# Attention on one core: GpSimd's pieces of a seven-tile batch handed out 2, 1, 1, 1, 1, 1 instead of 1, 1, 1, 1, 1, 2

## The chip, the cores and the metric

One core of a Trainium2 chip runs the whole kernel in one launch. The metric is the device time of one execution in microseconds (us), the median of several runs. Five engines work side by side and wait for each other by semaphores: TensorE (PE in the profile, its weight loads PEld), VectorE (DVE), ScalarE (ACT), GpSimd (POOL) and the queue that issues most DMAs (SP).

## The reference

Two kinds of layer alternate, spectral, attention, spectral, attention, each on a layer norm of x and with a residual. The change is in the attention layers, so only they are shown:

```python
B, S, D, H = 1, 2048, 512, 32          # Dh = 16, one key head shared by all 32 query heads
q = (x @ wq).reshape(B, S, H, Dh).transpose(0, 2, 1, 3)
k, v = x @ wk, x @ wv
scores = einsum("bhqd,bkd->bhqk", q, k) * Dh ** -0.5
o = einsum("bhqk,bkd->bhqd", softmax(scores), v)
return o.transpose(0, 2, 1, 3).reshape(B, S, H * Dh) @ wo
```

A spectral layer is an rfft2, a product with complex weights, and the inverse, written as matmuls.

## The kernel before

**Groups and tiles.** An attention layer works on 32 groups of 64 score tiles. A group `g` is four query heads and a block of 512 queries; its 64 tiles are 16 key blocks by 4 heads, each tile 128 keys by 512 queries. Every tile has to be exponentiated and multiplied with the values on TensorE (`pv`, L648).

**Two ways to the exponential.** Of the 64 tiles 45 go through ScalarE: TensorE writes scores into `sc` (L546), ScalarE's Exp reads them into `e` (L635), alternately three and two tiles at once. The other 19 go through VectorE in three batches, `DPOS`: 6, 7 and 6 tiles. VectorE turns a score tile `dv` into a 16-bit pattern by one multiply and add (`t_new`, L669, "the pass" below), whose bits are read as bf16. Such a pattern stands for a coarse exponential; it is made finer by adding four shifted copies of it, the images, with the weights `PH_W`. Image 0 is `t_new` itself. Images 1 and 2 are made by VectorE, the whole batch in one instruction (`s_new`, L684). Image 3 is made by GpSimd, one tile at a time: these are the pieces (`pool_new`, L688). Each tile of each image is a matmul of its own on TensorE.

**Steps.** The order is laid down by hand: a loop over steps `n`, one ScalarE Exp each, 18 steps for a group. In each step the instructions are recorded as `act_step`, `dv_score`, `dv_pass`, `image_step`, `pv_step`, and `chain()` pins the order on TensorE, ScalarE, VectorE and GpSimd. A batch `b` of group `g` has six image steps, k = 0 to 5 (`BSTEPS`), which begin at step 6b of the group. VectorE's image 1 comes at k = 0 and image 2 at k = 3 (`IMG`). The pieces were dealt out over k = 0 to 5 by `share`, which for seven tiles gives 1, 1, 1, 1, 1, 2.

**What a piece waits for.** `pace` (L550) makes each piece wait for the latest VectorE image that has been recorded, `image[0]`. For k = 0, 1, 2 that is image 1, for k = 3, 4, 5 it is image 2. Nothing else holds a piece back to its step.

**Who reads a piece.** `pv_step` multiplies the images' tiles in the order image 0, 1, 2, 3, two steps (`LAG`) after their own share of the six steps. Of a seven-tile batch, tiles 0 and 1 of image 3 are due at step 12 of the group and tiles 2 to 6 at step 13; in some steps a projection piece (`piece_at`) puts the `pv` matmuls off. TensorE works in order: while a `pv` matmul waits, the scores recorded behind it, of the next Exp among them, wait too.

**Other work beside.** In the first image step of the seven-tile batch GpSimd also normalises the group before (`od_new`, L580, recorded behind that step's pieces). VectorE transposes that result for two groups at once (`ot_new`, L586, only in groups of even number), just ahead of image 2 of the seven-tile batch. It also casts the next group's queries (`qt`, L376 and L380).

In what follows "image (1)" and "image (2)" of the seven-tile batch are VectorE's instructions at k = 0 and k = 3, "the next image" is image (1) of the third batch, six steps on from image (1), and piece 0 to piece 6 are GpSimd's.

Of the kernel before, what the change touches and what calls it, by code (L numbers as in the profile page):

```python
# [26 lines left out]
BSTEPS = 6  # L27
# [330 lines left out]
class Attention:  # L358
# [70 lines left out]
    def run(self, row_done, work, psums):  # L429
# [55 lines left out]
        share = lambda total, k: range(total * k // BSTEPS, total * (k + 1) // BSTEPS)  # L485
        due = {}
        for n0 in range(NS):
            lst = []
            if n0 in d_phase:
                g, b, k, tiles = d_phase[n0]  # L490
                for f in share(4 * len(tiles), k):
                    j, i = divmod(f, len(tiles))
# [57 lines left out]
        def pace(ins):  # L550
            if image[0] is not None:
                tc.add_manual_dep(ins.ins, image[0].ins.name, mybir.DependencyInfo(
                    mybir.DependencyClass.Sync, mybir.DependencyReason.DATA), reason="pace")
# [118 lines left out]
        def image_step(n):  # L672
            if n in d_phase:
                g, b, k, tiles = d_phase[n]
                src, nt = tb[(g, b)].bitcast(I16), len(tiles)
                if k == 0:
                    pool_new = work.tile([P, NBT, 512], I16, tag="SP", bufs=2)
                    sb[(g, b, 3)] = pool_new
                if k in IMG:
                    i = 1 + IMG.index(k)  # L680
                    s_new = work.tile([P, NBT, 512], I16, tag="S", bufs=3)
                    sb[(g, b, i)] = s_new
                    lo = POOL2 if i == 2 else 0
                    image[0] = nc.vector.tensor_scalar(out=s_new[:, lo:nt, :], in0=src[:, lo:nt, :], scalar1=PH_OFF[i], scalar2=None, op0=ALU.add)  # L684
                    if lo:
                        pace(nc.gpsimd.tensor_scalar(out=s_new[:, 0:lo, :], in0=src[:, 0:lo, :], scalar1=1.0, scalar2=PH_OFF[i], op0=ALU.mult, op1=ALU.add))
                for i in share(nt, k):
                    pace(nc.gpsimd.tensor_scalar(out=sb[(g, b, 3)][:, i, :], in0=src[:, i, :],  # L688
                                                 scalar1=1.0, scalar2=PH_OFF[3], op0=ALU.mult, op1=ALU.add))

# [13 lines left out]
        for n in range(NS + LAG + 2):  # L704
            now[0] = n
            act_step(n)
            dv = dv_score(n)
            for fn in pending:
                fn()
            del pending[:]  # L710
            if n in evict_at:
                evict(evict_at[n])
            dv_pass(n, dv)
            for fn in todo.pop(n, ()):
                fn()
            image_step(n)
            for fn in todo_pool.pop(n, ()):
                fn()
            pv_step(n)
            if n in piece_at:  # L720
                piece(*piece_at[n])
            chain()
# [447 lines left out]
```

## Time and profile before

| | us |
|---|---|
| median of 3 runs | 1563.37 (1562.22 to 1563.38) |
| the profiled execution's own time | 1565.87 |
| its span, first to last instruction | 1564.1 |
| busy in the span: ScalarE | 1442.9 (92%) |
| VectorE | 1420.6 (91%) |
| TensorE | 1349.6 (86%) |
| GpSimd | 797.0 (51%) |

The two attention layers take from about 110 to 790 us and from about 870 to 1555 us of the span; the spectral layers lie ahead of each. A busy share is an average: what a stage could gain is read from its own waits. In a row of the timeline stand the start, the time taken, engine, line, operation, tiles and count; the bracket behind it is the idle time ahead of it and what ended that. Instructions of one kind that follow each other are merged into one row with a count.

### The profile page before, as it was taken

The page shows a single profiled execution, that of the slowest core. Times are in us where ns is not written, and L with a number is a line of the kernel's source. Part 1 is how long each engine was busy: PE and PEld are TensorE (multiplying, and loading weights), DVE is VectorE, ACT ScalarE, POOL GpSimd, SP SyncE. Part 2 cuts the span into 40 slices and gives each one's busy share as a digit, 9 for nine tenths or more (in the row PEclk, how much of TensorE's full clock was granted, in tenths as well). Part 3 has the DMA queues.
Part 4 walks back from the last instruction along what each step waited for, and adds up shares of the span by engine and source line. Part 5 has one row for each costly group of instructions (what it writes and reads, how often), then busy time and mean ns, then how long its engine had stood idle before and what let it go on. Part 6 is the DMA issues. An engine that isn't in the chain of part 4 may idle for free.

```text
span 1564.1 us, 33013 instructions
## 1 busy us (share of the span) xinstructions
PE 1349.6 (86%) x13145; PEld 429.5 (27%) x13252; DVE 1420.6 (91%) x2279; ACT 1442.9 (92%) x1361; POOL 797.0 (51%) x1310
## 2 busy tenths in 40 slices
PE   5888888899888988898889788888998899889987
PEld 2442222222222222222234322222222222222222
DVE  6687999999999999999987889999999999999995
ACT  6659999999999999999965799999999999999996
POOL 1003555565656655665600055556556656666564
PEclk9997999999999999999999899999999999999998
DMA  8000000000000000000010000000000000000000
GB/s 278 16 1 1 2 2 1 1 1 2 1 2 1 1 1 2 1 2 1 1 41 1 1 1 2 2 1 5 5 2 5 5 4 5 5 5 5 5 5 18
DMA packets 13198, 17.21 MB, mean 11 GB/s; under 512 B 5748, under 2 KB 10484, under 8 KB 12788
## 3 DMA queue, kind: packets, MB, share of 16 engines
q1 hardware_dynamic: 12660, 14.05, 2.7%
q8 instruction: 103, 1.69, 0.4%
q0 software_dynamic: 384, 1.05, 0.2%
q14 instruction: 51, 0.42, 0.1%
HBM read 13.00 MB, written 2.10 MB: 10 GB/s over the span
## 4 chain that ended last, share of the span: by engine, by line
DVE 35%; ACT 31%; issue 14%; PE 12%; POOL 4%; DVEq 0%; POOLq 0%; ACTq 0%
ACT e L635 30%; DVE t_new L669 16%; DVE s_new L684 9%; POOL pool_new L688 4%; PE pv_new L648 4%; PE sc L546 3%; DVE st L105 1%; PE new L203 1%; DVE o L565 1%; DVE qt L376 1%; DVE ot_new L586 1%; PE dv L546 1%; PE new L294 1%; PE new L242 1%; DVE dst L353 1%
## 5 line engine op out<-in xcount | busy, mean ns | idle before, releaser
L635 ACT ACTIVATE e<-sc 128x1536 bf16<-128x1536 f32 (+1 forms) x1158 | 1316.6, 1293 | 21.7 <-PE dv L546 17.4
L688 POOL TENSOR_SCALAR pool_new<-t_new 128x512 int16<-128x512 int16 x1204 | 748.5, 644 | 719.9 <-DVE s_new L684 630.4
L669 DVE TENSOR_SCALAR t_new<-dv 128x512 uint16<-128x512 f32 x1204 | 791.5, 677 | 76.3 <-PE dv L546 61.7
L648 PE MATMUL pv_new<-e,vaug 128*32 128x512 bf16 x2892 | 595.6, 389 | 0.0
L546 PE MATMUL sc<-qt,KT 32*128 32x512 bf16 x2892 | 459.2, 388 | 115.0 <-ACT e L635 108.5
L546 PE MATMUL dv<-qt,KT 32*128 32x512 bf16 x1204 | 455.3, 387 | 21.8 <-DVE t_new L669 20.2
L648 PE MATMUL pv_new<-s_new,vaug 128*32 128x512 bf16 x2408 | 422.5, 386 | 5.9 <-DVE s_new L684 5.9
L684 DVE TENSOR_SCALAR s_new<-t_new 128x3584 int16<-128x3584 int16 (+1 forms) x380 | 386.3, 1017 | 0.1
L648 PE MATMUL pv_new<-pool_new,vaug 128*32 128x512 bf16 x1204 | 299.8, 387 | 20.8 <-POOL pool_new L688 20.8
L546 PEld LDWEIGHTS <-KT 32*128 32x128 bf16 x4096 | 156.7, 91 | 561.0 <-issue 559.4
L648 PEld LDWEIGHTS <-vaug 128*32 128x32 bf16 x7708 | 154.3, 94 | 399.3 <-issue 368.3
L648 PE MATMUL pv_new<-t_new,vaug 128*32 128x512 bf16 x1204 | 232.7, 387 | 0.0
L370 PE MATMUL ps<-xz,wq_sb 128*128 128x512 bf16 x186 | 61.5, 386 | 4.1 <-DVE t_new L669 0.4
L565 DVE STREAM_TRANSPOSE o<-pv_new 128x512 f32<-128x512 f32 x64 | 45.2, 706 | 12.2 <-PE pv_new L648 12.2
L203 PE MATMUL new<-tab_F,xz 128*128 128x512 bf16 x186 | 48.2, 404 | 3.5 <-DVE xz L167 3.3
L376 DVE TENSOR_SCALAR qt<-ps,kq 128x512 bf16<-128x512 f32 x62 | 46.0, 742 | 1.2 <-PE ps L370 1.2
L105 DVE BATCH_NORM_STATS2 st<-x_sb 128x6 f32<-128x512 bf16 x64 | 42.9, 671 | 3.6 <-DMA x_sb<-in_A_x_dram 3.5
L580 POOL TENSOR_TENSOR od_new<-o,den 128x256 bf16<-128x256 f32 x62 | 38.5, 620 | 0.0
L267 DVE TENSOR_TENSOR m<-x_new,wt 128x1024 bf16<-128x1024 bf16 x32 | 20.7, 687 | 14.3 <-ACT x_new L243 14.3
L243 ACT CAST x_new<-new 128x1024 bf16<-128x1024 f32 x16 | 16.2, 1012 | 18.4 <-PE new L242 17.0
L370 PEld LDWEIGHTS <-wq_sb 128*128 128x128 bf16 x256 | 22.0, 97 | 31.5 <-issue 16.7
L336 PE MATMUL new<-G_new,t_new 128*128 128x512 bf16 x128 | 29.9, 379 | 0.5 <-DVE G_new L303 0.4
(106 smaller groups left out, 582.0 us busy)
## 6 DMA issues: line engine op xcount, KB each, us to landing
tab_F<-const_F SPq DMA_DIRECT2D x5, 640.0 KB, 11.7
x_sb<-in_A_x_dram SPq DMA_DIRECT2D x4, 512.0 KB, 4.8
t_new<-const_IE SPq DMA_DIRECT2D x2, 1024.0 KB, 7.3
rt<-in_A_w_r_dram SPq DMA_DIRECT2D x1, 1028.0 KB, 8.4
rt<-in_A_w_i_dram SPq DMA_DIRECT2D x1, 1028.0 KB, 12.7
t_new<-const_IO SPq DMA_DIRECT2D x2, 512.0 KB, 3.3
out_dram<-x_sb SPq DMA_DIRECT2D x8, 128.0 KB, 2.0
out_dram<-x_sb POOLq DMA_DIRECT2D x8, 128.0 KB, 2.3
```

What stands on the lines that cost most here:

```text
L105: self.nc.vector.bn_stats(st, x_ap)
L203: self.mm(ps, lhsT=z, rhs=tab, start=start and i == 0, stop=stop and i == len(mms) - 1)
L370: self.nc.tensor.matmul(ps, lhsT=self.aw["wq"][:, c, hg, :], rhs=self.xT[:, c, 4 * qb:4 * qb + 4, :].rearrange("d k p -> d (k p)"), start= ...
L376: self.nc.vector.tensor_scalar(out=qt, in0=ps, scalar1=self.kq[:, 1:2], scalar2=None, op0=ALU.mult)
L546: nc.tensor.matmul(dst, lhsT=KT[hs, kc * P:(kc + 1) * P], rhs=QT[g][hs, :], start=True, stop=True)
L565: nc.vector.transpose(out=o.rearrange("p c j -> p (c j)"), in_=ps)
L580: return engine.tensor_tensor(out=turned_od[g // 2][:, :, half], in0=o[:, :, 0:DH], in1=den.unsqueeze(2).broadcast_to([P, 16, DH]), op=ALU ...
L635: nc.scalar.activation(out=e[:, 0:na, :], in_=sc[:, 0:na, :], func=ACT.Exp, scale=SCALE)
L648: nc.tensor.matmul(pv[g][32 * h:32 * h + 32, :], lhsT=vaug[:, max(j, 0), kc, :], rhs=rhs, start=(first_pv[(g, h)] == u), stop=(last_pv[(g, ...
L669: nc.vector.tensor_scalar(out=tb[(g, b)][:, i, :], in0=dv, scalar1=T_MUL, scalar2=T_ADD, op0=ALU.mult, op1=ALU.add)
L684: image[0] = nc.vector.tensor_scalar(out=s_new[:, lo:nt, :], in0=src[:, lo:nt, :], scalar1=PH_OFF[i], scalar2=None, op0=ALU.add)
L688: pace(nc.gpsimd.tensor_scalar(out=sb[(g, b, 3)][:, i, :], in0=src[:, i, :], scalar1=1.0, scalar2=PH_OFF[3], op0=ALU.mult, op1=ALU.add))
```

## The change

In `image_step` the pieces of a step are no longer taken from `share(nt, k)`, which rounds down, but from the same division rounded up. For six tiles both give one piece for each step. For seven tiles the second piece of k = 5 moves to k = 0: pieces 0 and 1 are recorded in k = 0, and pieces 2 to 6 in k = 1 to 5, each of them one step earlier than before or in the same step. In terms of the image they wait for, pieces 0 to 2 waited for image (1) and pieces 3 to 6 for image (2); now pieces 0 to 3 wait for image (1) and pieces 4 to 6 for image (2). On GpSimd `od_new` now stands behind piece 1 instead of behind piece 0. The order on TensorE, VectorE, ScalarE and the DMA queue is what it was.

```diff
-                for i in share(nt, k):
+                for i in range(-(-nt * k // BSTEPS), -(-nt * (k + 1) // BSTEPS)):
                     pace(nc.gpsimd.tensor_scalar(out=sb[(g, b, 3)][:, i, :], in0=src[:, i, :],
                                                  scalar1=1.0, scalar2=PH_OFF[3], op0=ALU.mult, op1=ALU.add))
```

## The prediction

> **What bounds the kernel now.** I began with the busy time by stretch, for the two attention layers, then asked who waits for whom over the whole span.
>
> ```profile
> sum 1315.00, PE 1147.74 PEld 337.83 DVE 1228.58 ACT 1290.21 POOL 762.02; mean PE 573.87 PEld 168.92 DVE 614.29 ACT 645.10 POOL 381.01
> ...
> PE sc L546 <- ACT e L635: 108.5, 359, 0.6
> ...
> ACT e L635 <- PE dv L546: 17.4, 24, 1.5
> ...
> PE pv_new L648 <- POOL pool_new L688: 20.8, 24, 1.3
> ```
>
> Over 1315 us of attention (110 to 745 and 870 to 1550 of the span) ScalarE is busy 1290, or 98%; VectorE 93%, TensorE 87%, GpSimd 58%. TensorE's commonest wait is for ScalarE's Exp to free a score buffer. So ScalarE sets the pace, and the kernel gains only where ScalarE is made to wait. It waited for TensorE 24 times, and 24 times TensorE waited for one of GpSimd's pieces. Equal counts don't make a cause, so I followed one group in the timeline: group 6 of the first attention layer, an even one, with image (1) at 254.97.
>
> ```profile
> 254.97 1.08 DVE L684 TENSOR_SCALAR s_new<-t_new 128x3584 int16<-128x3584 int16 x1
> ...
> 258.69 0.70 DVE L586 STREAM_TRANSPOSE ot_new<-od_new 128x512 bf16<-128x512 bf16 x1
> 259.31 1.05 DVE L684 TENSOR_SCALAR s_new<-t_new 128x3584 int16<-128x3584 int16 x1
> 260.28 1.87 DVE L669 TENSOR_SCALAR t_new<-dv 128x512 uint16<-128x512 f32 x3
> 262.08 0.96 DVE L684 TENSOR_SCALAR s_new<-t_new 128x3072 int16<-128x3072 int16 x1
> ...
> 256.24 0.62 POOL L688 TENSOR_SCALAR pool_new<-t_new 128x512 int16<-128x512 int16 x1 [1.38 <-PE ps L370]
> 256.82 0.62 POOL L580 TENSOR_TENSOR od_new<-o,den 128x256 bf16<-128x256 f32 x1
> 257.40 1.24 POOL L688 TENSOR_SCALAR pool_new<-t_new 128x512 int16<-128x512 int16 x2
> 260.44 3.06 POOL L688 TENSOR_SCALAR pool_new<-t_new 128x512 int16<-128x512 int16 x4 [1.80 <-DVE s_new L684]
> ...
> 263.56 0.38 PE L648 MATMUL pv_new<-pool_new,vaug 128*32 128x512 bf16 x1 [0.98 <-POOL pool_new L688]
> ...
> 262.71 1.04 ACT L635 ACTIVATE e<-sc 128x1024 bf16<-128x1024 f32 x1
> 264.39 1.45 ACT L635 ACTIVATE e<-sc 128x1536 bf16<-128x1536 f32 x1 [0.63 <-PE dv L546]
> ```
>
> Read it from the bottom. Between two Exps ScalarE sat idle 0.63 us. The new scores were late because TensorE had stood 0.98 us in front of a `pv` matmul that reads a piece; it was there at 262.58 and got the piece at 263.5. GpSimd's row of four pieces (3 to 6) ends at 260.44 + 3.06 = 263.50. Four undisturbed pieces take 2.36 us (the row of group 5 below), so 0.70 was lost, and the place shows: the next image starts at 262.08 and ends at 263.04, and piece 6, queued at about 262.19, finished only 0.46 us after that end. Pieces don't run beside that image.
>
> The same stretch of group 5, an odd group, goes differently:
>
> ```profile
> 234.59 1.08 DVE L684 TENSOR_SCALAR s_new<-t_new 128x3584 int16<-128x3584 int16 x1
> ...
> 238.31 1.08 DVE L684 TENSOR_SCALAR s_new<-t_new 128x3584 int16<-128x3584 int16 x1
> 239.31 1.28 DVE L669 TENSOR_SCALAR t_new<-dv 128x512 uint16<-128x512 f32 x2
> 240.80 0.69 DVE L669 TENSOR_SCALAR t_new<-dv 128x512 uint16<-128x512 f32 x1 [0.21 <-PE dv L546]
> 241.41 1.24 DVE L684 TENSOR_SCALAR s_new<-t_new 128x3072 int16<-128x3072 int16 x1
> ...
> 237.03 1.24 POOL L688 TENSOR_SCALAR pool_new<-t_new 128x512 int16<-128x512 int16 x2
> 239.48 2.36 POOL L688 TENSOR_SCALAR pool_new<-t_new 128x512 int16<-128x512 int16 x4 [1.21 <-DVE s_new L684]
> ...
> 237.67 1.16 ACT L635 ACTIVATE e<-sc 128x1024 bf16<-128x1024 f32 x1
> ...
> 242.34 1.04 ACT L635 ACTIVATE e<-sc 128x1024 bf16<-128x1024 f32 x1
> ...
> 243.24 1.49 ACT L635 ACTIVATE e<-sc 128x1536 bf16<-128x1536 f32 x1
> ```
>
> Here piece 6 was first (start about 241.22, end 241.84), and the next image, started at 241.41, took 1.24 instead of 0.96. VectorE lost 0.28, TensorE had its piece, and the same two Exps follow each other in 0.90 us instead of 1.68. So in even groups ScalarE loses 0.78 us at this place.
>
> **How often.** The first and the last of these waits:
>
> ```profile
> 180.59 0.38 PE L648 MATMUL pv_new<-pool_new,vaug 128*32 128x512 bf16 x1 [0.98 <-POOL pool_new L688]
> ...
> 1523.87 0.38 PE L648 MATMUL pv_new<-pool_new,vaug 128*32 128x512 bf16 x1 [0.98 <-POOL pool_new L688]
> ```
>
> I count 18 of 0.98 us among the 24, nine a layer: groups 2, 4, 6, 8, 14, 16, 22, 24 and 30. In the other even groups an output projection stands at that step and puts the `pv` off. 18 x 0.98 = 17.6 of the 20.8 us; 1.3 more is one wait at the very end, told of below.
>
> **The change, part by part.** No instruction is added or removed. The steps don't hold a piece back, only the images do: in the rows above pieces 1 and 2, and 3 to 6, run without a gap though they belong to different steps. So the change amounts to moving piece 3 from behind image (2) to behind image (1), and `od_new` back by one piece.
>
> *Even groups.* Behind image (1) GpSimd now runs pieces 0 and 1, `od_new`, pieces 2 and 3. The first four of these five end where the old four did, at 257.40 + 1.24 = 258.64; piece 3 follows to 259.22. Image (2) starts at 259.31: no meeting, 0.09 us to spare. `od_new` ends at about 258.0, and its reader, the transpose, starts at 258.69: not late. Behind image (2) three pieces are left; they end where piece 5 ended, about 262.22. The next image starts 0.14 us before that end, as it did, and lost nothing by it (0.96). Piece 6 is there at 262.22 instead of 263.50, and TensorE comes for it at 262.58: the wait goes, with 0.36 to spare. What is late next? After the next image the even group stands as the odd one does now: that image ends 0.33 us after the Exp that began at 262.71, in group 5 0.31 after the one at 242.34, and group 5 goes on without loss. So I take the whole 0.78: 18 x 0.78 = -14.0 us. Its bounds are ScalarE's idle time alone, 18 x 0.63 = 11.3, and all of TensorE's wait, 17.6.
>
> *Odd groups.* There is no transpose, and image (2) comes 3.72 us after image (1) instead of 4.34. Piece 3 would start at about 238.23 (the pair at 237.03 ends at 238.27, and GpSimd's starts lie 0.04 ahead of the end before) and image (2) at 238.31; piece 3 would run to about 238.85. Who is first by 0.08 us blocks the other. A row with the same order and nearly the same distance is in the last group:
>
> ```profile
> 1539.49 1.48 DVE L684 TENSOR_SCALAR s_new<-t_new 128x3584 int16<-128x3584 int16 x1
> ...
> 1538.83 1.20 POOL L688 TENSOR_SCALAR pool_new<-t_new 128x512 int16<-128x512 int16 x2
> ```
>
> The second of that pair started at about 1539.41, 0.08 before the image, and ended 0.54 after the image's start; the image took 1.48 instead of 1.08. So image (2) is 0.40 us later in odd groups, to about 239.80. The first two passes behind it move by 0.40, the third, which waited 0.21 for TensorE, by about 0.1; the next image starts at about 241.52, meets only the last 0.15 of piece 6, as in the even group, and ends at 242.48 instead of 242.65. The cover is VectorE's slack against ScalarE there: in the even group image (2) ends at 260.36, 2.35 us before the Exp at 262.71; in the odd group it would end 2.54 before its Exp at 242.34. The even group is later and pays nothing:
>
> ```profile
> 258.05 1.16 ACT L635 ACTIVATE e<-sc 128x1024 bf16<-128x1024 f32 x1
> ```
>
> From this Exp to the one at 262.71 are 4.66 us, in the odd group from 237.67 to 242.34 4.67. So I cost the delay at nothing; without that cover it costs 0.40 in each of 32 odd groups, 12.8 us. If the image were first after all, piece 3 would wait and nothing else in this sum changes.
>
> The Trainium skill, "SBUF — State Buffer", section "Who interferes with whom", says that VectorE in a two-port mode and GpSimd share one pair of ports, and that whoever issues first holds it for the whole instruction while the other is fully blocked. The trace agrees in both orders (a piece 0.70 us longer in group 6, an image 0.40 us longer in the last group).
>
> *A small loss.* The even groups, which follow an undisturbed odd one, pay a little at their queries' cast that odd ones don't:
>
> ```profile
> 256.64 1.65 ACT L635 ACTIVATE e<-sc 128x1536 bf16<-128x1536 f32 x1
> ...
> 236.32 1.59 ACT L635 ACTIVATE e<-sc 128x1536 bf16<-128x1536 f32 x1
> ```
>
> To the Exp behind it are 1.41 us in the even group and 1.35 in the odd one. Once even groups run undisturbed too, I expect the 0.06 in the odd ones behind them: some 16 x 0.06 = +1.0 us, between 0 and 1.0.
>
> *The last group.*
>
> ```profile
> 1544.97 0.58 PE L648 MATMUL pv_new<-pool_new,vaug 128*32 128x512 bf16 x1 [1.31 <-POOL pool_new L688]
> ...
> 1520.00:1543.00 23.00, 18.57 (x207) 5.59 (x204) 21.08 (x31) 22.37 (x21) 15.07 (x24) 1.00 0.02 8
> 1546.00:1550.00 4.00, 4.00 (x30) 0.70 (x27) 0.00 (x0) 3.21 (x3) 2.41 (x5) 0.50 0.00 0
> ```
>
> TensorE waits 1.31 us for piece 6; with one piece fewer behind image (2) I take 1.0 of it off. From there the granted clock is 0.50 instead of 1.00 and TensorE is busy all 4.00 us of that stretch. If the pause is what brings the clock down, a shorter one may keep it up: 4.00 against ScalarE's 3.21 gives about 1.0 us more. Together -2.0, between 0 and -3.0.
>
> The Trainium skill, "TensorE: Matmul & The Clock Gate", section "What's actually happening", has the clock fall after an idle window of about 3.4 us. By it a pause of 1.31 would not have done it, and the second microsecond would stay where it is: the sum would be 1.0 higher.
>
> **The sum.** -14.0 + 1.0 - 2.0 = -15.0 us. The profiled execution took 1565.87 us, its span 1564.1; the difference of 1.8 lies around the span and isn't touched. It is 2.5 above the median 1563.37, and the terms are waits of 0.1 to 1.3 us that don't scale with that, so I take the sum off the median: 1563.4 - 15.0 = 1548.4 us.
>
> **Rivals.** *The delay in odd groups is paid after all.* It decides once the slack of the even groups doesn't hold for odd ones. Fully paid: 1548.4 + 12.8 = 1561.2, half 1554.8. For it: VectorE is 93% busy. Against: the 4.66 and 4.67 us above. Chance 0.11.
>
> *Another wait takes the place of piece 6.* TensorE would stop at the next thing, say VectorE's pass behind the next image. Half of the 14.0 left: 1555.4; all of it: 1562.4. Against: group 5, which has that lag already. Chance 0.08.
>
> *Slower: GpSimd's longer run holds up the transpose, and VectorE becomes the bound.* In even groups piece 3 (258.60 to 259.22) now runs beside the transpose at 258.69. Blocked like an image, the transpose would lose about 0.40, image (2) would move 0.40 beyond a lag shown to be harmless, and with the odd groups' 0.40 all 64 groups would pay: 25.6 - 15.0 = +10.6, 1574.0 us. It decides above 15.0 / 64 = 0.23 us paid per group. No run shows this transpose beside a piece; the nearest is the other one, from PSUM:
>
> ```profile
> 250.85 0.70 DVE L565 STREAM_TRANSPOSE o<-pv_new 128x512 f32<-128x512 f32 x1
> ...
> 249.92 1.78 POOL L688 TENSOR_SCALAR pool_new<-t_new 128x512 int16<-128x512 int16 x3 [2.60 <-DVE s_new L684]
> ```
>
> It ran beside pieces in its usual 0.70. Chance 0.06.
>
> *The change does nothing,* because the pieces would come in the same order behind the same images. Against: the order that `pace` lays down. Chance 0.01.
>
> **How the numbers follow.** The forecast has 0.74. Its own range takes the bounds of its terms: -17.6 + 0 - 3.0 gives 1543 at the far end and -11.3 + 1.0 + 0 gives 1553; both ends at once are unlikely, so 1545 to 1553. Reaching to 1557 takes in the half-paid cases of the first two rivals and leaves out about 2 in 10. What a measurement of this kernel can tell from no change is 0.2%, or 3.1 us; faster means below 1560.2. Faster: 0.74 + 0.08 of the first rival + 0.05 of the second = 0.87. Same: 0.03 + 0.03 + 0.01 = 0.07. Slower: 0.06.
>
> **What would show it.** Right: the waits of `pv` for pieces fall from 24 to about 6 and from 20.8 to about 3 us; the Exps of group 6 that stood 1.68 apart stand 0.90 apart; image (2) of odd groups takes 1.48, the next image 0.96; `pool_new` has no 1.3 us piece at the next image in even groups; the last stretch keeps a higher clock. Wrong: TensorE waits longer for VectorE's passes (`PE dv L546 <- DVE t_new`), `ot_new` above 0.70, or ScalarE's waits for TensorE no fewer than 24.

## The result and the profile after

The change takes the kernel from 1562.8 us (median of 4 runs, 1560.6 to 1563.4) to 1545.95 us (4 runs, 1544.7 to 1547.6). The ratio is 0.9895, with a 95% interval of 0.9878 to 0.9912: 16.9 us less, between 14 and 19. The forecast was 15.0 less, 1548.4. The profiled execution after took 1544.67 us, its span 1542.9.

First the waits over the whole span, after the change: engine, line and what it waited for, then us in total, times, and the longest.

```profile
PE sc L546 <- ACT e L635: 112.6, 340, 0.8
...
PE dv L546 <- DVE t_new L669: 15.6, 62, 0.8
...
PE pv_new L648 <- DVE s_new L684: 5.9, 30, 0.2
...
ACT e L635 <- PE dv L546: 5.1, 5, 1.3
...
PE pv_new L648 <- POOL pool_new L688: 1.3, 3, 0.5
```

TensorE's waits for pieces fell from 24 to 3 and from 20.8 to 1.3 us, and ScalarE's waits for TensorE with them, from 24 to 5 and from 17.4 to 5.1. Of TensorE's other waits in these layers only the one for ScalarE's Exp grew, from 108.5 to 112.6 us, which costs nothing while ScalarE sets the pace. The one for VectorE's passes is 15.6 us; before it was

```profile
PE dv L546 <- DVE t_new L669: 20.2, 74, 0.8
```

Now the same even group as in the prediction, group 6 of the first attention layer, in the timeline after:

```profile
255.39 1.05 DVE L684 TENSOR_SCALAR s_new<-t_new 128x3584 int16<-128x3584 int16 x1
256.36 1.87 DVE L669 TENSOR_SCALAR t_new<-dv 128x512 uint16<-128x512 f32 x3
258.15 0.96 DVE L684 TENSOR_SCALAR s_new<-t_new 128x3072 int16<-128x3072 int16 x1
...
252.31 1.20 POOL L688 TENSOR_SCALAR pool_new<-t_new 128x512 int16<-128x512 int16 x2 [1.37 <-PE ps L370]
253.47 0.62 POOL L580 TENSOR_TENSOR od_new<-o,den 128x256 bf16<-128x256 f32 x1
254.06 1.24 POOL L688 TENSOR_SCALAR pool_new<-t_new 128x512 int16<-128x512 int16 x2
256.51 1.78 POOL L688 TENSOR_SCALAR pool_new<-t_new 128x512 int16<-128x512 int16 x3 [1.22 <-DVE s_new L684]
...
258.78 1.04 ACT L635 ACTIVATE e<-sc 128x1024 bf16<-128x1024 f32 x1
...
259.69 1.49 ACT L635 ACTIVATE e<-sc 128x1536 bf16<-128x1536 f32 x1
```

Two pieces, `od_new` and two pieces stand behind image (1) and end at 255.30, just ahead of image (2) at 255.39. Three are left behind it and end at 258.29; they meet only the first 0.14 us of the next image, which takes its 0.96. The two Exps that stood 1.68 us apart stand 0.91 apart.

Group 5, an odd one:

```profile
234.38 1.48 DVE L684 TENSOR_SCALAR s_new<-t_new 128x3584 int16<-128x3584 int16 x1
235.79 1.90 DVE L669 TENSOR_SCALAR t_new<-dv 128x512 uint16<-128x512 f32 x3
237.60 0.95 DVE L684 TENSOR_SCALAR s_new<-t_new 128x3072 int16<-128x3072 int16 x1
...
233.68 1.24 POOL L688 TENSOR_SCALAR pool_new<-t_new 128x512 int16<-128x512 int16 x2
```

Piece 3 holds image (2) up, which takes 1.48 instead of 1.08, and the next image takes 0.95 instead of 1.24. The contact hasn't gone away; it has moved to a place where it costs no ScalarE time.

### The profile page after: what moved, and what is told of

Read it like the earlier page. It is cut to its first block, busy times and chain, and to the rows that moved or that the text cites. A ratio compares the mean times of both kernels' runs of the same rounds, so it can differ in the third digit from the quotient of the medians.

```text
span 1542.9 us, 33013 instructions
## 1 busy us (share of the span) xinstructions
PE 1347.2 (87%) x13145; PEld 431.1 (28%) x13252; DVE 1424.9 (92%) x2279; ACT 1439.1 (93%) x1361; POOL 778.3 (50%) x1310
## 4 chain that ended last, share of the span: by engine, by line
ACT 36%; DVE 36%; issue 15%; PE 10%; POOL 0%; DVEq 0%; POOLq 0%; ACTq 0%
ACT e L635 35%; DVE t_new L669 16%; DVE s_new L684 9%; PE sc L546 2%; PE pv_new L648 2%; DVE st L105 1%; DVE o L565 1%; PE new L203 1%; DVE qt L376 1%; DVE ot_new L586 1%; PE new L294 1%; PE dv L546 1%; PE new L242 1%; DVE dst L353 1%; DVE x_sb L353 1%
## 5 line engine op out<-in xcount | busy, mean ns | idle before, releaser
L688 POOL TENSOR_SCALAR pool_new<-t_new 128x512 int16<-128x512 int16 x1204 | 727.6, 626 | 722.6 <-DVE s_new L684 633.4
L648 PE MATMUL pv_new<-e,vaug 128*32 128x512 bf16 x2892 | 584.8, 387 | 0.0
L546 PE MATMUL sc<-qt,KT 32*128 32x512 bf16 x2892 | 456.0, 385 | 119.8 <-ACT e L635 112.6
L546 PE MATMUL dv<-qt,KT 32*128 32x512 bf16 x1204 | 452.0, 385 | 18.6 <-DVE t_new L669 15.6
L684 DVE TENSOR_SCALAR s_new<-t_new 128x3584 int16<-128x3584 int16 (+1 forms) x380 | 393.7, 1036 | 0.1
L243 ACT CAST x_new<-new 128x1024 bf16<-128x1024 f32 x16 | 16.2, 1012 | 18.4 <-PE new L242 17.0
```

The source lines that it names most:

```text
L546: nc.tensor.matmul(dst, lhsT=KT[hs, kc * P:(kc + 1) * P], rhs=QT[g][hs, :], start=True, stop=True)
L648: nc.tensor.matmul(pv[g][32 * h:32 * h + 32, :], lhsT=vaug[:, max(j, 0), kc, :], rhs=rhs, start=(first_pv[(g, h)] == u), stop=(last_pv[(g, ...
```

## The experiments

Each kernel differs from the kernel before only in the lines shown. Times are medians, beside runs of the kernel before on the same chip (1562.14 us for the first four, 1562.43 for the last three); ratios are to those.

**New hand-out in even groups only.**

```diff
-                for i in share(nt, k):
+                for i in range(-(-nt * k // BSTEPS), -(-nt * (k + 1) // BSTEPS)) if g % 2 == 0 else share(nt, k):
```

> The new hand-out in even groups, the old one in odd groups. If the gain is piece 6's wait in 18 even groups (0.78 us each), most of it comes here: -14.0, less some 16 x 0.07 = 1.1 that the odd groups behind them then pay at the queries' cast; the tail (group 31 of each layer is odd) and the odd groups keep their old times: -13, about 1550 us for 1562.8, and the profile has no 0.98 us wait of pv for a piece, but still the 1.3 us one in the last group with the clock at 0.50 behind it. If the odd groups' shorter next image brings the gain (VectorE as the bound): 32 groups unchanged there, about 1560 or more.

Measured: 1548.69 us, ratio 0.9906 (0.9884 to 0.9928), 13.5 less. Its waits:

```profile
ACT e L635 <- PE dv L546: 5.8, 6, 1.5
PE pv_new L648 <- POOL pool_new L688: 2.4, 3, 1.3
```

The even groups carry the gain, as piece 6's theory has it and the rival of VectorE as the bound does not. What was left, the 1.3 us wait of the last group, was expected too; the clock behind it is taken up below.

**New hand-out in odd groups only.** The same line with `if g % 2` instead.

> The new hand-out in odd groups, the old one in even groups. By the theory of piece 6 in even groups the 18 waits of 0.98 us stay. Gains are left in the 12 odd groups with an output projection (0.16 us of ScalarE's time each in the new kernel's trace, 2.0 us) and in the last group (its 1.3 us wait and the clock behind it, 2 to 4 us): 1557 to 1559 us. If the odd groups' image (2), 0.40 us later, were paid (32 x 0.40 = 12.8), the time would be 1570 or more. If even groups don't matter, 1546 as with the whole change.

Measured: 1560.66 us, ratio 0.9986 (0.9975 to 0.9998): 1.5 us less in the medians, where 4 to 6 were expected. The waits of the even groups are still there:

```profile
PE pv_new L648 <- POOL pool_new L688: 19.6, 24, 1.0
ACT e L635 <- PE dv L546: 17.0, 24, 1.5
```

Neither rival holds: the odd groups' later image (2) is not paid (no 12.8 us more), and even groups do matter. The expectation was too high by 2.5 us or more. The share of the odd groups with a projection came as expected: from the first to the last of the nine 0.98 us waits of the first layer are 579.35 us here and 580.30 before, in the second layer 0.93 less. What the medians lack is the last group's share, which hangs on the clock and stays open, as told below. The two halves add up to 15.0 us, the whole change gave 16.9 beside other runs; that lies within the intervals.

**Doubled step moved, four pieces behind image (1).** Handed out 1, 1, 2, 1, 1, 1:

```diff
+                hand = (1, 1, 2, 1, 1, 1)
-                for i in share(nt, k):
+                for i in range(sum(hand[:k]), sum(hand[:k + 1])) if nt == 7 else share(nt, k):
```

> Seven pieces handed out 1, 1, 2, 1, 1, 1: piece 3 is recorded in step 2, od_new stands behind piece 0 again, but as in the change four pieces wait for image (1) and three for image (2). If only the image that a piece waits for matters, this is the whole change again: 1546 us, within 2 us of it. If the recorded step or od_new's place mattered, it would lie between 1546 and 1563.

Measured: 1546.27 us, ratio 0.9890 (0.9868 to 0.9913). The whole change again, with another doubled step and with `od_new` back in its old place. Three of the four times recorded for this kernel (1545.19, 1546.7 and 1547.57 us, the last that of the execution profiled here) stand in the record of the change as well, so the two medians are not independent; the five different times lie between 1544.7 and 1547.6. What is this kernel's own is its trace: `od_new` stands behind one piece and ahead of three, and the waits for pieces are gone as in the change (L689 is L688, moved by the added line):

```profile
PE pv_new L648 <- POOL pool_new L689: 1.4, 3, 0.6
```

**Doubled step moved, three pieces behind image (1).** `hand = (1, 1, 1, 2, 1, 1)`.

> Seven pieces handed out 1, 1, 1, 2, 1, 1: the doubled step moves from step 5 to step 3, yet three pieces still wait for image (1) and four for image (2). If only the image matters, nothing changes: 1563 us, within 2 us of the kernel before, with 18 waits of 0.98 us. If it helped to record pieces 4 to 6 a step earlier, the time would fall by up to the 17 us of the change.

Measured: 1562.66 us, ratio 1.0002 (0.9988 to 1.0016), with 23 waits of `pv` for a piece, 20.6 us in all. Recording pieces 4 to 6 a step earlier does nothing. As far as these runs show, the six-step hand-out is a way of writing only two numbers, how many pieces wait for each image: 3 and 4 before, 4 and 3 after.

**Piece 6 left out, old hand-out.**

```diff
-                for i in share(nt, k):
+                for i in share(min(nt, 6), k):
...
-                    rhs = img[:, i, :].bitcast(BF)
+                    rhs = img[:, min(i, 5) if j == 3 else i, :].bitcast(BF)
```

> The old hand-out with one piece fewer: GpSimd leaves piece 6 of each seven-tile batch out, and TensorE's matmul of that tile reads piece 5 in its place (so image 3 of one tile in 64 is another tile's). Order and count on the other engines stay. If TensorE's wait in even groups is for piece 6, it goes without any moving of piece 3: 18 x 0.78 = -14.0, +1.1 in the odd groups behind, -2.0 in the odd groups with an output projection (the next image no longer 0.28 late), -1 to -3 in the last group: 1545 to 1548 us, the same as the change. It also shows what image (2) of the odd groups, 0.40 us later in the change and undisturbed here, costs: nothing, if the two times agree within 2 us. If TensorE waits for VectorE's next image or a pass there, the time stays near 1562.

Measured: 1545.95 us, ratio 0.9896 (0.9881 to 0.9911). Here image (2) has no piece beside it. Its groups of 3584 elements, in this kernel and then after the change (128 instructions, images (1) and (2) together; the last number ahead of the second bar is the mean in ns):

```profile
L684 DVE TENSOR_SCALAR s_new<-t_new 128x3584 int16<-128x3584 int16 x128 | 138.2, 1079 | 0.0
```

```profile
L684 DVE TENSOR_SCALAR s_new<-t_new 128x3584 int16<-128x3584 int16 x128 | 150.1, 1172 | 0.0
```

So VectorE spends 11.9 us more on these images in the change, and the two kernels take the same time, within about 2 us. That is the step of the prediction that costed the 12.8 us of delay at nothing, shown by leaving the delay out (and by the kernel with the new hand-out in odd groups only, which has the delay and is no slower than before). It also shows that the change has all that piece 6 had to give: without the piece the kernel is no faster.

**Five pieces behind image (1).** `hand = (2, 2, 1, 1, 1, 0)`, the next step in the same direction.

> Handed out 2, 2, 1, 1, 1, 0: five pieces wait for image (1), two for image (2). In even groups piece 4 now starts about 0.13 us before image (2), which then takes 1.40 instead of 1.05; in odd groups image (2) takes 1.48 as in the change, and piece 4 waits behind it (some 1.4 us). The next image meets no piece. So the one new cost is image (2) 0.35 us later in 32 even groups, beyond any lag seen so far. If VectorE's slack covers that too: 1546 us. If all of it is paid: 1546 + 11 = 1557. I expect part of it: 1548 to 1552.

Measured: 1554.28 us, ratio 0.9951 (0.9936 to 0.9965): 8.1 less than before, and some 8 more than the change. Group 6:

```profile
256.27 1.44 DVE L684 TENSOR_SCALAR s_new<-t_new 128x3584 int16<-128x3584 int16 x1
...
254.94 1.83 POOL L689 TENSOR_SCALAR pool_new<-t_new 128x512 int16<-128x512 int16 x3
...
257.43 1.02 ACT L635 ACTIVATE e<-sc 128x1024 bf16<-128x1024 f32 x1
...
258.59 1.45 ACT L635 ACTIVATE e<-sc 128x1536 bf16<-128x1536 f32 x1
```

and of its waits:

```profile
PE pv_new L648 <- DVE s_new L684: 17.7, 30, 0.6
```

Piece 4, the last of the three, ends at 256.77 and makes image (2), started at 256.27, 0.39 us longer. TensorE, which waits 0.2 us for this image in 30 even groups before and after the change (5.9 us in all), now waits 0.6, and the Exps at 257.43 and 258.59 stand 1.16 apart. Before, the same pair stood 0.90 apart, as it does after the change:

```profile
260.48 1.02 ACT L635 ACTIVATE e<-sc 128x1024 bf16<-128x1024 f32 x1
...
261.38 1.46 ACT L635 ACTIVATE e<-sc 128x1536 bf16<-128x1536 f32 x1
```

30 x 0.26 = 7.8 us, nearly all of the loss. So VectorE's slack has an edge in even groups: a wait of 0.2 us is free, 0.6 costs 0.26. In odd groups, where the change puts its delay, TensorE doesn't come to wait for image (2): all 30 of these waits are in even groups, before and after. I had expected 1548 to 1552, too little.

**Two pieces behind image (1), five behind image (2).** `hand = (1, 1, 0, 2, 2, 1)`.

> Handed out 1, 1, 0, 2, 2, 1: two pieces wait for image (1), five for image (2), the other way from the change. By the theory in even groups two pieces (5 and 6) stand behind the next image and piece 6 comes 0.58 us later than before: waits of 1.56 instead of 0.98, 18 x 0.58 = +10. In odd groups piece 5 is now the one that holds the next image up, and piece 6 is blocked behind that image and comes about 0.9 us after TensorE: some 14 to 18 odd groups lose about 0.7: +10 to +13. Together 1582 to 1587 us against 1562. If only the balance between the two halves mattered and not whom a piece meets, the loss would be near the 16 us that the step from 3/4 to 4/3 gave.

Measured: 1604.27 us, ratio 1.0262 (1.0239 to 1.0285): 41.8 us slower, where 20 to 25 were expected. The waits in even groups were as expected; group 4 of the first layer in the timeline, then the waits over the span:

```profile
224.82 0.38 PE L648 MATMUL pv_new<-pool_new,vaug 128*32 128x512 bf16 x1 [1.57 <-POOL pool_new L689]
```

```profile
PE pv_new L648 <- POOL pool_new L689: 54.4, 40, 1.6
ACT e L635 <- PE dv L546: 47.9, 56, 1.7
```

The wait of 1.57 us was forecast as 1.56, and 40 waits in place of 24 show odd groups waiting now: 18 of them, 1.29 or 1.35 us each, where 0.9 was forecast. ScalarE waits 30.5 us longer for TensorE than before. Where the clock stays up, its wait is 1.23 us in an even group instead of 0.63 and 0.63 to 0.69 in an odd one instead of nothing; 18 of each are 22 us, as forecast. What was not expected is TensorE's clock; the stretches below belong to this kernel (start and end, length, busy time of PE, PEld, DVE, ACT and POOL, granted clock, then the DMAs):

```profile
223.00:225.00 2.00, 0.43 (x7) 0.10 (x3) 1.31 (x2) 1.43 (x2) 2.00 (x3) 1.00 0.00 0
225.00:229.00 4.00, 4.00 (x38) 0.79 (x34) 2.75 (x4) 2.87 (x3) 1.93 (x4) 0.59 0.00 0
...
110.00:1500.00 1390.00, 1206.90 (x11837) 359.10 (x11929) 1261.29 (x1985) 1296.04 (x1189) 751.44 (x1197) 0.96 0.01 3
```

Behind the pause the clock is 0.59 for 4 us, TensorE is busy all of them, and ScalarE does 2.87 us of work. Over 110 to 1500 us the clock is 0.96 here and 0.99 in the kernel before. The clock fell behind 18 of the 40 waits. What such a fall costs can be read where it didn't happen: from group 6's wait to that of group 7 are 21.17 us (268.21 to 289.38), and in nine other places with a fall behind the even group's wait 21.40 to 22.64, 0.8 more on average. 18 x 0.8 = 14 us is an estimate of the clock's share; with the 22 us of waits that makes some 36 of the 41.8.

## Why the prediction was right

**The bound and the cause.** ScalarE lost time because TensorE stood in front of piece 6, and piece 6 was late because it met the next image. Three runs show it: leaving the piece out gives the same 1545.95 us, the even groups alone give 13.5 us, and a longer row of pieces at that place makes the wait 1.57 instead of 0.98.

**Even groups, -14.0.** Measured 13.5 with the new hand-out in even groups only, which has the small loss of the odd groups in it, +1.0 by forecast. In the traces two groups take 40.75 us with it instead of 41.49 (from TensorE's wait for image (2) in group 2 to that in group 4), 0.74 less where 0.78 - 0.06 was forecast. The small loss came too: after the change the Exp at the queries' cast of group 5 starts 1.40 us ahead of the next one instead of 1.35. Where the prediction asked what is late next, nothing was.

**Odd groups, 0.** The image's 0.40, the next image's 0.15 of contact and the harmlessness came as told. One thing was missed, in the gaining direction: in the 12 odd groups that have an output projection, ScalarE gained. The Exps of group 9 two steps apart, before:

```profile
326.21 1.49 ACT L635 ACTIVATE e<-sc 128x1536 bf16<-128x1536 f32 x1
...
328.70 1.45 ACT L635 ACTIVATE e<-sc 128x1536 bf16<-128x1536 f32 x1
```

and after:

```profile
320.81 1.49 ACT L635 ACTIVATE e<-sc 128x1536 bf16<-128x1536 f32 x1
...
323.14 1.45 ACT L635 ACTIVATE e<-sc 128x1536 bf16<-128x1536 f32 x1
```

2.49 us became 2.33: 12 x 0.16 = 1.9 us. The prediction had the next image end 0.17 earlier there and gave it no worth, since it looked at a group without a projection. With the odd groups alone the kernel gained 1.5 us, about this.

**The last group, -2.0.** Its wait went from 1.31 to 0.29 us, the forecast 1.0, and the clock stayed at 1.00:

```profile
1526.75 0.38 PE L648 MATMUL pv_new<-pool_new,vaug 128*32 128x512 bf16 x1 [0.29 <-POOL pool_new L688]
```

```profile
1527.00:1531.00 4.00, 3.40 (x42) 1.07 (x38) 0.52 (x1) 4.00 (x5) 3.90 (x6) 1.00 0.00 0
```

The second microsecond, the clock's, was too small for an execution in which the clock falls. From this wait's end to the end of the span are 19.1 us before (1544.97 to 1564.1), with the clock down, and 16.2 after (1526.75 to 1542.9), with the clock up: 3.0 us, where the prediction took 1.0 from a single stretch of 4 us. But this share can't be booked to the change in every run. The kernel with the old hand-out in odd groups has the same pause of 1.32 us there, its clock stayed up, and from there to the end of its span, at 1547.0, are 15.9 us:

```profile
1531.15 0.38 PE L648 MATMUL pv_new<-pool_new,vaug 128*32 128x512 bf16 x1 [1.32 <-POOL pool_new L688]
```

```profile
1531.00:1535.00 4.00, 3.46 (x42) 1.12 (x41) 0.00 (x0) 3.35 (x4) 3.59 (x7) 1.00 0.00 0
```

So the same pause is followed by a lower clock in one execution and not in another. This term was right in its first microsecond and is open in its second, between nothing and 3.0: there is one trace of each kernel, and the one of the kernel before is of an execution slower than the median. The odd groups alone, which take this pause away and gained only 1.5 us in all, speak for less than 2.0 in the median. That the whole sum came within 2 us of the 16.9 is luck in part: the missed 1.9 is about the difference, and this term could have moved it either way.

**The rivals.** The delay in odd groups is not paid: the kernel without piece 6 has no such delay and takes the same time. Nothing took the place of piece 6. The transpose beside piece 3 kept its time, the open point of the slower rival: it ran from 254.76, piece 3 from about 254.68 to 255.30.

```profile
254.76 0.70 DVE L586 STREAM_TRANSPOSE ot_new<-od_new 128x512 bf16<-128x512 bf16 x1
```

The Trainium skill, "SBUF — State Buffer", section "Who interferes with whom", says that a VectorE instruction with one SBUF input and outside the two-port modes doesn't contend with GpSimd. This row agrees, if the transpose is such an instruction; its mode isn't in the trace.

## What to carry to other kernels

A share of 50% busy on an engine says nothing of whom its instructions meet: look in the timeline for instructions that get longer in one order and let the other engine wait in the opposite one, and count how many of the shorter ones fit between two of the longer. A contact that can't be removed can be moved to the side that has slack, here from a piece that TensorE waits for to an image that it reaches later. The slack has an edge: four pieces behind the first image fitted, a fifth gave back 8 of the 17 us, and two instead of three cost 42.

## What the hardware showed that I had not expected

In these traces TensorE's granted clock falls to half after pauses of 1 to 1.6 us, but not after each of them. In the kernel with two pieces behind image (1) it fell behind 16 of the 18 pauses of 1.57 us and behind one of the 18 of 1.29 or 1.35. At the usual wait of 0.98 us for piece 6 it fell 3 times in 54: never in the trace of the kernel before, twice in that with the doubled step moved and three pieces behind image (1), and once in the kernel with the new hand-out in odd groups only. There it fell in the second layer's last even group:

```profile
1521.01 0.58 PE L648 MATMUL pv_new<-pool_new,vaug 128*32 128x512 bf16 x1 [0.98 <-POOL pool_new L688]
```

```profile
1517.00:1520.90 3.90, 2.83 (x30) 0.66 (x28) 3.90 (x6) 3.90 (x4) 3.01 (x4) 1.00 0.00 0
1521.00:1524.30 3.30, 3.29 (x27) 0.61 (x26) 1.30 (x3) 2.16 (x3) 2.30 (x4) 0.50 0.15 46
```

TensorE was busy 2.83 of the 3.90 us ahead of the fall, the pause with them, and the matmul behind the pause took 0.58 us where it took 0.38 in group 6 before. There the clock stayed up, and TensorE had been busy just as long:

```profile
259.60:263.50 3.90, 2.79 (x27) 0.62 (x25) 3.90 (x6) 3.90 (x4) 3.06 (x5) 1.00 0.00 0
```

So neither the pause's length nor the busy time ahead of it decides alone; the fall is only commoner behind the longest pauses. The Trainium skill, "TensorE: Matmul & The Clock Gate", section "What's actually happening", has the clock set by windows of about 3.4 us that run freely and don't start with the kernel. That would fit the two outcomes of equal pauses, but the windows themselves don't show in the traces. That section of the Trainium skill names an idle window of about 3.4 us as what brings the clock down; here the clock fell after pauses of less than half of that. What decides is left open. In practice a wait of TensorE can cost more than its own length: in the kernel with three pieces behind image (1) and the doubled step moved, two groups from one wait of 0.98 us to the next took 42.41 us where the clock fell (264.55 to 306.96) and 41.49 where it didn't.
